# The product with v of some heads: from split one-pass matmuls on the whole array to plain fp32 matmuls on two halves of it

## The chip, the cores and the metric

The kernel runs on one core of a Trainium2 chip. The metric is the device time of one execution in microseconds (us). The engines are named as in the profile: PE is TensorE's matmul, PEld its weight load, DVE VectorE, ACT ScalarE, POOL GpSimd, and SP SyncE, whose queue issues almost all transfers.

## What is computed

Attention with a hashed mask, and then a mixture of four experts that all tokens pass. There are B = 2 batches, H = 8 heads, S = 768 positions and head size D = 64; the experts take rows of 512 and have 1024 hidden units.

```
mask = q_bucket[:, :, :, None] == k_bucket[:, :, None, :]     # 6 sign bits of q @ proj and of k @ proj
scores = where(mask, q @ k.T / sqrt(D), -1e9)
attn = exp(scores - max); attn = attn / (sum(attn) + 1e-9)
x = (attn @ v), heads side by side                            # [1536, 512]
out = sum over e of p[:, e] * (relu(x @ w1[e]) @ w2[e])
```

Everything is fp32. The array multiplies fp32 data in two types here: `F32R`, one pass with fewer bits of each operand kept, and plain `F32`. To reach fp32 with `F32R` operands the kernel splits each operand into a high part and a low part and adds the part-products.

## The kernel before, in words

**The attention loop.** The function `attention` walks over 96 steps i, one for each query tile t of 128 rows, of 16 heads in order (batch 0 first). In each step the string `ORDER = "THXVMSEYNRP"` sets which stages are issued and in which order, each for the tile that lies its own lag behind: S (scores, L401 and L403, and the masked minimum on DVE, L408), E (exponential on ACT, L424), N and R (sums of rows and their reciprocals, through DRAM), P (preparing the next head, and loading the one after), M (scaling by the reciprocals).

**The two ways of turning p.** The product with v needs p transposed. The first 9 heads (b * H + h below `LIGHT_FROM` = 9) do it on PE: stage T transposes with the identity (L470), ACT copies the high part (L474) and DVE makes the low part (L475). The last 7 heads, called light, go through DRAM. Stage X (three steps after S) transposes blocks of 32 x 32 on DVE (L489) and writes them to a DRAM tile `scr` (L493). Stage Y (four steps after) reads it back with four gathering transfers (L502) into a tile `ptlo`. Stage H (six steps after) copies its high part into `pthi` on ACT (L515) and subtracts it in place on POOL (L516).

**The product with v.** Two query tiles form a group g of 256 columns, so a head has three groups. `split_v` (on POOL, L353 and L356, at the head's step 4) makes from v a tile `vv` whose 128 columns per chunk of keys are the high part (64) beside the low part (64). Stage V (`stage_v`, L526) does six matmuls of 256 moving columns with the high part of p in one step (part 0), and six with the low part in the next step (part 1), all into one PSUM bank `pv`. Then ACT copies the 64 rows of the other part into `xtmp` (L546), and DVE adds them to the head's own 64 rows (L551 for light heads, L558 for the others). `LAG_VL` = 7 sets part 0 of light heads seven steps after S.

**The experts beside it.** The experts of batch 0 (`moe`: first layer L775 to L777, second layer L715 to L717) are issued in between the attention steps of batch 1. The ratio is fixed in the program: each stage yields a cost (654 for each part of V, 652 for S, 1960 or 2600 for pieces of the experts), and attention steps are issued until their sum has caught up. After that follow the experts of batch 1 (`moe_fast`). Every engine takes its instructions in the order in which they are written.

**Memory.** `load_v` (L210, on SP's queue) brings v of a head two heads ahead into the pool `ld` (tag `tv`, two slots); `vv` has two slots in the pool `vp`; `pthi` and `ptlo` have two each. PSUM tiles named `one` share four banks (`pv`, `mps`).

Of the kernel before, what the change touches and what calls it, by code (L numbers as in the profile page):

```python
# [8 lines left out]
F32 = mybir.dt.float32  # L9
F32R = mybir.dt.float32r  # L10
ACTF = mybir.ActivationFunctionType
ALU = mybir.AluOpType
PSUM = bass.MemoryType.PSUM

P = 128
# [20 lines left out]
WARM = 2  # L36
W_STEP = 12
PREP_AT = 0
ORDER = "THXVMSEYNRP"
LIGHT_FROM = 9  # L40
LAG_VL = 7
DRAIN = 1000
LAG_X = 3
LAG_Y = 4
LAG_H = 6
SPLIT_FIRST = 3


# [1 line left out]
def tile_lsh_attention__then__domain_moe(  # L50
# [11 lines left out]
    nc = tc.nc  # L62
    B, H, S, D = q.shape
    NB = proj.shape[1]
    E, DM, F = w1.shape
    NT = S // P
# [8 lines left out]
    GN = G * P  # L75
# [8 lines left out]
    ld = ctx.enter_context(tc.tile_pool(name="ld", bufs=2))  # L84
    stk = ctx.enter_context(tc.tile_pool(name="stk", bufs=2))
    vp = ctx.enter_context(tc.tile_pool(name="vp", bufs=2))
# [3 lines left out]
    ptp = ctx.enter_context(tc.tile_pool(name="ptp", bufs=2))  # L90
# [13 lines left out]
    def one(name):  # L104
        return ps1.tile([P, 512], F32, tag="one", name=name)
# [93 lines left out]
    def load_qk(b, h):  # L199
        if in_blocks(b, h):  # L200
            load_blocks(b, h)
            return
        t = ld.tile([P, NT, 2, D], F32, tag="tqk", name="tqk")
        for i, src in enumerate((q, k)):
            nc.sync.dma_start(out=t[:, :, i, :], in_=src[b, h].rearrange("(p c) d -> p c d", c=NT))
        loaded[0, b, h] = t

    def load_v(b, h):
        t = ld.tile([P, NT, D], F32, tag="tv", name="tv")
        nc.sync.dma_start(out=t, in_=v[b, h].rearrange("(p c) d -> p c d", c=NT))  # L210
        loaded[1, b, h] = t

# [133 lines left out]
    vvs = {}  # L346

    def split_v(b, h):
        tv = loaded.pop((1, b, h))
        vv = vp.tile([P, NT, P], F32R, tag="vv", name="vv")  # L350
        vvs[b, h] = vv
        hi, lo = (0, D) if h % 2 == 0 else (D, 0)
        nc.gpsimd.tensor_scalar(  # L353
            out=vv[:, :, hi : hi + D], in0=tv, scalar1=1.0, scalar2=1.0, op0=ALU.mult, op1=ALU.mult
        )
        nc.gpsimd.tensor_tensor(  # L356
            out=vv[:, :, lo : lo + D], in0=tv, in1=vv[:, :, hi : hi + D].bitcast(F32), op=ALU.subtract
        )
# [3 lines left out]
    for j in range(KD):  # L362
        t = xp.tile([P, 2, S], F32R, tag=f"x{j}", name="xs0")
# [14 lines left out]
    pts = {}  # L378
    pvs = {}
    xf = {}  # L380

    def light(b, h):
        return b * H + h >= LIGHT_FROM
# [46 lines left out]
    rows = {}  # L430
# [46 lines left out]
    pxs = {}  # L477
# [27 lines left out]
            )  # L505
        pxs[b, h, g] = (px, lo)

    def stage_h(b, h, g):
        px, lo = pxs.pop((b, h, g))
        hi = ptp.tile([P, NT, GN], F32R, tag="pthi", name="pthi")  # L510
        fh = hi.rearrange("p c n -> p (c n)")
        fl = lo.rearrange("p c n -> p (c n)")
        for a in range(2):
            sl = slice(a * S, (a + 1) * S)
            nc.scalar.activation(fh[:, sl], px[:, sl], ACTF.Copy)  # L515
            nc.gpsimd.tensor_tensor(out=fl[:, sl], in0=px[:, sl], in1=fh[:, sl].bitcast(F32), op=ALU.subtract)  # L516
        view = [x.rearrange("p (a c q) -> p c a q", c=NT, q=32) for x in (fh, fl)]
        pts[b, h, g] = view

    def stage_v(b, h, g, part):  # L520
        vv = vvs[b, h]
        if part == 0:
            pvs[b, h, g] = one("pv")
        ps = pvs[b, h, g]
        for c in range(NT):
            nc.tensor.matmul(  # L526
                ps[:, :GN].rearrange("p (a q) -> p a q", q=32) if light(b, h) else ps[:, :GN],
                vv[:, c],
                pts[b, h, g][part][:, c],
                start=part == 0 and c == 0,  # L530
                stop=part == 1 and c == NT - 1,
            )
        if part == 0:
            return
        pts.pop((b, h, g))
        pvs.pop((b, h, g))
        j, odd = divmod(h, 2)
        if b:
            x = xraw[:, j, g * GN : (g + 1) * GN]
        else:  # L540
            if not odd:
                xf[b, j, g] = xs.tile([P, GN], F32, tag=f"xf{g}", name="xf", bufs=1)
            x = xf[b, j, g]
        mine, other = (slice(0, D), slice(D, P)) if not odd else (slice(D, P), slice(0, D))
        tmp = xs.tile([P, GN], F32, tag="xtmp", name="xtmp")
        nc.scalar.activation(tmp[mine], ps[other, :GN], ACTF.Copy)  # L546
        if XADD_POOL and b == 0:
            nc.scalar.activation(x[mine], ps[mine, :GN], ACTF.Copy)
            nc.gpsimd.tensor_tensor(out=x[mine], in0=x[mine], in1=tmp[mine], op=ALU.add)
        elif light(b, h):  # L550
            nc.vector.tensor_tensor(  # L551
                out=x[mine].rearrange("p (t a q) -> p a t q", t=G, q=32),
                in0=ps[mine, :GN].rearrange("p (a t q) -> p a t q", t=G, q=32),
                in1=tmp[mine].rearrange("p (a t q) -> p a t q", t=G, q=32),
                op=ALU.add,
            )
        else:
            nc.vector.tensor_tensor(out=x[mine], in0=ps[mine, :GN], in1=tmp[mine], op=ALU.add)  # L558
# [20 lines left out]
    def attention():  # L579
        n = len(seq)  # L580
        prep = [iter(())]

        def stage_light(f, j):
            if 0 <= j < n and light(*seq[j][:2]) and j % G == G - 1:
                b, h, t = seq[j]
                f(b, h, t // G)

        def do(op, i):
            if op == "N":
                j = i - LAG_N  # L590
                if 0 <= j < n:
                    stage_n(*seq[j])
            elif op == "R":
                j = i - LAG_R
                if 0 <= j < n:
                    stage_r(*seq[j])
            elif op == "T":
                j = i - LAG_T
                if 0 <= j < n and not light(*seq[j][:2]):
                    stage_t(*seq[j])  # L600
                    return 654
            elif op == "X":
                stage_light(stage_x, i - LAG_X)
            elif op == "H":
                stage_light(stage_h, i - LAG_H)
            elif op == "Y":
                stage_light(stage_y, i - LAG_Y)
            elif op == "S":
                if i < n:
                    b, h, t = seq[i]  # L610
                    if t == 0:
                        x = hseq.index((b, h))
                        prep[0] = prep_head(*hseq[x + 1]) if x + 1 < len(hseq) else iter(())
                    stage_s(b, h, t)
                    return 652
                return DRAIN
            elif op == "V":
                c = None
                for il, lag in enumerate((LAG_V, LAG_VL)):
                    for part in range(G):  # L620
                        j = i - lag - part
                        if 0 <= j < n and j % G == G - 1 and light(*seq[j][:2]) == bool(il):
                            b, h, t = seq[j]
                            stage_v(b, h, t // G, part)
                            c = 654 + (c or 0)
                return c
            elif op == "M":
                for g in range(NT // G):
                    for lag, last in ((LAG_M + g, False), (LAG_V + 1 + G * g + G - NT, True)):
                        j = i - lag  # L630
                        if 0 <= j < n and j % NT == NT - 1 and seq[j][1] % 2:
                            if (seq[j][:2] == (0, H - 1)) == last:
                                stage_m(*seq[j][:2], g)
            elif op == "E":
                j = i - LAG_E
                if 0 <= j < n:
                    stage_e(*seq[j])
            elif op == "P":
                if i < n:
                    b, h, t = seq[i]  # L640
                    c = next(prep[0], None) if t >= PREP_AT else None
                    x = hseq.index((b, h))
                    if t == QK_AT and x + 2 < len(hseq):
                        load_qk(*hseq[x + 2])
                    if t == 4:
                        split_v(b, h)
                        if x + 2 < len(hseq):
                            load_v(*hseq[x + 2])
                    return c
            return None  # L650

        for i in range(n + max(LAG_V, LAG_VL) + G + 1):
            for op in ORDER:
                c = do(op, i)
                if c is not None:
                    yield c
# [338 lines left out]
    with tc.manual_schedule():  # L995
# [7 lines left out]
        i = 0  # L1003
# [17 lines left out]
        for b in range(B):  # L1021
            dm = da = 0.0
            for c in (moe_fast if b else moe)(b, b * NU):
                dm += c
                while da < dm * ATT_PACE * n_att / n_moe:
                    x = next(att, None)
# [34 lines left out]
```

## Time and profile before

| | |
|---|---|
| time, median of 3 runs | 735.47 us (735.18 to 736.24) |
| the profiled execution | 735.63 us, of which 733.9 are the span from first to last instruction |
| busy share of the span | PE 99%, PEld 90%, DVE 70%, ACT 49%, POOL 47% |
| mean granted TensorE clock | 1.000 of full speed |
| product with v, all heads (L526) | 576 matmuls, 88.5 us busy |

Busy times of PE are sums of printed durations without overlap; one matmul is printed with its whole latency, and the next one starts before it ends. A time per instruction is therefore better read from one start to the next. Idle time of an engine other than the one that sets the end costs nothing by itself.

### The profile page before, as it was taken

Reading aid. Unit: us, or ns where it says so; the run is one execution under the profiler, and the core shown is the slowest. Engines: PE = TensorE matmul, PEld = TensorE weight load, DVE = VectorE, ACT = ScalarE, POOL = GpSimd, SP = SyncE. Lnnn points to the kernel's source line nnn. Section 1 sums busy time; section 2 is a strip of 40 time slices with the busy share of each in tenths; the row PEclk is TensorE's granted clock in tenths of the full one; section 3 lists DMA queues with packets and bytes.
Section 4 is the critical chain, followed back from the end, with each engine's and each line's share of the span. In section 5 each row is a group of like instructions: output and inputs, shape, how many; then the busy total and the mean of one; then the engine's idle time right before and its main releaser. Section 6 shows DMA issues by size and latency. Waiting matters only on the chain.

```text
span 733.9 us, 11306 instructions
## 1 busy us (share of the span) xinstructions
PE 723.1 (99%) x4060; PEld 663.6 (90%) x4060; DVE 516.2 (70%) x898; ACT 356.0 (49%) x702; POOL 345.9 (47%) x298
## 2 busy tenths in 40 slices
PE   8899999999999999999999999999999999999998
PEld 6899899998998989989899999898988989899896
DVE  6899999947577766766766433878668586686863
ACT  6999899744444454535444211443435234353430
POOL 6142715422576666675756733844334242343420
PEclk9999999999999999999999999999999999999999
DMA  4555464444989897987776412142121221212202
GB/s 97 152 128 121 92 159 102 115 106 120 239 207 239 240 222 206 223 236 205 215 212 208 112 58 84 56 147 87 58 58 59 84 87 48 68 58 82 92 0 87
DMA packets 77272, 94.86 MB, mean 129 GB/s; under 512 B 38712, under 2 KB 51960, under 8 KB 77216
## 3 DMA queue, kind: packets, MB, share of 16 engines
q1 hardware_dynamic: 76192, 93.81, 46.8%
q8 instruction: 32, 0.52, 0.3%
q10 hardware_dynamic: 1024, 0.33, 0.2%
q14 instruction: 24, 0.20, 0.1%
HBM read 62.68 MB, written 19.71 MB: 112 GB/s over the span
## 4 chain that ended last, share of the span: by engine, by line
PE 87%; DVE 6%; ACT 3%; DMA 2%; issue 1%; POOL 1%; SPq 0%; ACTq 0%; DVEq 0%; POOLq 0%
PE mps L717 12%; PE mps L715 12%; PE mps L716 12%; PE pv L526 6%; PE mps L775 6%; PE mps L777 6%; PE mps L776 6%; PE sps L403 3%; PE sps L401 3%; DVE p L408 3%; PE mps L931 2%; PE mps L927 2%; PE mps L930 2%; PE ptps L470 2%; DVE ptlo L475 2%; PE hps L317 2%
## 5 line engine op out<-in xcount | busy, mean ns | idle before, releaser
L717 PE MATMUL mps<-w2hi,hl 128*128 128x512 f32 (+1 forms) x388 | 151.1, 389 | 0.0
L715 PE MATMUL mps<-w2hi,hh 128*128 128x512 f32 (+1 forms) x388 | 151.0, 389 | 0.0
L716 PE MATMUL mps<-w2lo,hh 128*128 128x512 f32 (+1 forms) x388 | 150.7, 388 | 0.0
L709 DVE SCALAR_TENSOR_TENSOR acc<-mps,pe,acc 128x512 f32<-128x512 f32 (+1 forms) x85 | 63.0, 741 | 64.4 <-PE mps L717 64.4
L424 ACT ACTIVATE p<-p,nb 128x768 f32<-128x768 f32 x96 | 89.6, 933 | 26.4 <-DVE p L408 25.8
L516 POOL TENSOR_TENSOR ptlo<-ptlo,pthi 128x768 fp32r<-128x768 f32 x42 | 77.4, 1864 | 48.8 <-ACT pthi L515 44.8
L408 DVE TENSOR_SCALAR_CACHE_REDUCE p<-sps 128x768 f32<-128x768 f32 x96 | 90.6, 945 | 1.5 <-PE sps L403 0.7
L913 POOL TENSOR_TENSOR w2lo<-ws,w2hi 128x512 fp32r<-128x512 f32 x32 | 40.8, 1297 | 105.9 <-ACT w2hi L912 105.9
L717 PEld LDWEIGHTS mps<-w2hi,hl 128*128 128x128 f32 x388 | 72.9, 188 | 17.1 <-DVE hl L946 1.3
L775 PE MATMUL mps<-xs,w1hi 128*128 128x384 f32 x256 | 86.5, 338 | 0.0
L777 PE MATMUL mps<-xs,w1lo 128*128 128x384 f32 x256 | 86.1, 336 | 0.0
L776 PE MATMUL mps<-xs,w1hi 128*128 128x384 f32 x256 | 86.0, 336 | 0.0
L782 ACT ACTIVATE hh<-mps 128x384 fp32r<-128x384 f32 x64 | 31.4, 490 | 112.2 <-PE mps L777 112.0
L716 PEld LDWEIGHTS mps<-w2lo,hh 128*128 128x128 f32 x388 | 73.0, 188 | 13.5
L715 PEld LDWEIGHTS mps<-w2hi,hh 128*128 128x128 f32 x388 | 72.9, 188 | 13.0
L783 DVE SCALAR_TENSOR_TENSOR hl<-mps,hh 128x384 fp32r<-128x384 f32 x64 | 35.4, 553 | 52.2 <-ACT hh L782 51.7
L685 POOL TENSOR_TENSOR w1lo<-ws,w1hi 128x512 fp32r<-128x512 f32 x32 | 42.5, 1332 | 43.6 <-DVE w1hi L692 17.0
L685 POOL TENSOR_TENSOR w2lo<-ws,w2hi 128x512 fp32r<-128x512 f32 x32 | 42.6, 1333 | 37.5 <-DVE w2hi L692 25.9
L475 DVE TENSOR_TENSOR ptlo<-ptps,pthi 128x384 fp32r<-128x384 f32 x108 | 54.5, 545 | 7.5 <-ACT pthi L474 7.2
L872 POOL TENSOR_TENSOR w1lo<-ws,w1hi 128x512 fp32r<-128x512 f32 x24 | 38.3, 1612 | 35.9 <-ACT w1hi L868 29.2
L401 PE MATMUL sps<-ah,q 128*128 128x384 f32 x192 | 50.1, 342 | 2.3 <-DVE p L408 2.1
L403 PE MATMUL sps<-k,al 76*128 76x384 f32 x192 | 50.4, 342 | 0.7 <-DVE k L263 0.4
(139 smaller groups left out, 1558.0 us busy)
## 6 DMA issues: line engine op xcount, KB each, us to landing
ws<-in_moe_w_dram SPq DMA_DIRECT2D x64, 512.0 KB
scr<-t SPq DMA_DIRECT2D x21, 768.0 KB
ptlo<-scr SPq DMA_DIRECT2D x84, 192.0 KB
q<-ah SPq DMA_DIRECT2D x28, 192.0 KB
tv<-in_v_dram SPq DMA_DIRECT2D x16, 192.0 KB
k<-ah SPq DMA_DIRECT2D x15, 192.0 KB
rdb<-row SPq DMA_DIRECT2D x15, 192.0 KB
out_dram<-acc SPq DMA_DIRECT2D x11, 256.0 KB
```

The lines of the kernel that those rows point to most:

```text
L401: nc.tensor.matmul(ps[:, i, :NH], q1[:, sl], k1[:, i * NH : (i + 1) * NH], start=True, stop=False)
L403: nc.tensor.matmul(ps[:, i, :NH], q2[0:MQE, sl], k2[0:MQE, i * NH : (i + 1) * NH], start=False, stop=True)
L408: nc.vector.tensor_scalar(out=two(pt), in0=ps[:, :, :NH], scalar1=MASKED, scalar2=MASKED, op0=ALU.min, op1=ALU.min, accum_out=nb,)
L424: nc.scalar.activation(pt, pt, ACTF.Exp, bias=nb, scale=-1.0, accum_out=dens[b, h, r][:, o : o + 1])
L516: nc.gpsimd.tensor_tensor(out=fl[:, sl], in0=px[:, sl], in1=fh[:, sl].bitcast(F32), op=ALU.subtract)
L685: nc.gpsimd.tensor_tensor(out=lo[:, c - 1], in0=st[c - 1], in1=hi[:, c - 1].bitcast(F32), op=ALU.subtract)
L715: nc.tensor.matmul(ps, hh[:, ts], w2hi[:, f, cs], start=n == 0, stop=False)
L716: nc.tensor.matmul(ps, hh[:, ts], w2lo[:, f, cs], start=False, stop=False)
L717: nc.tensor.matmul(ps, hl[:, ts], w2hi[:, f, cs], start=False, stop=n == FC - 1)
L775: nc.tensor.matmul(ps[:, :SB], w1hi[:, kk, fs], xhi[b, kk][:, sl], start=kk == 0, stop=False)
L776: nc.tensor.matmul(ps[:, :SB], w1hi[:, kk, fs], xlo[b, kk][:, sl], start=False, stop=False)
L777: nc.tensor.matmul(ps[:, :SB], w1lo[:, kk, fs], xhi[b, kk][:, sl], start=False, stop=kk == KD - 1)
```

## The change

For light heads stage H goes away, and v is not split. The tile `ptlo`, as the transfers bring it, is the moving operand in plain fp32, and v as loaded is the standing operand, 64 columns per chunk of keys. The six chunks go by turns to the left and the right half of the array's columns (`tile_position` (0, 0) and (0, 64)), so that the even chunks add up in PSUM rows 0 to 63 and the odd ones in rows 64 to 127. The add of the two halves after it (L546, L551) is as before. All six matmuls are issued in the step of part 0, and none in the step of part 1. Because v as loaded is now read by PE, `load_v` puts it by turns into `tv` and `vv` slots. The 9 other heads stay as they are.

```diff
--- before.py
+++ after.py
@@ -36,13 +36,12 @@
 WARM = 2
 W_STEP = 12
 PREP_AT = 0
-ORDER = "THXVMSEYNRP"
+ORDER = "TXVMSEYNRP"
 LIGHT_FROM = 9
 LAG_VL = 7
 DRAIN = 1000
 LAG_X = 3
 LAG_Y = 4
-LAG_H = 6
 SPLIT_FIRST = 3
 
 
@@ -206,7 +205,9 @@
         loaded[0, b, h] = t
 
     def load_v(b, h):
-        t = ld.tile([P, NT, D], F32, tag="tv", name="tv")
+        x = b * H + h - LIGHT_FROM
+        pool, tag = (vp, "vv") if x >= 0 and x // 2 % 2 else (ld, "tv")
+        t = pool.tile([P, NT, D], F32, tag=tag, name="tv")
         nc.sync.dma_start(out=t, in_=v[b, h].rearrange("(p c) d -> p c d", c=NT))
         loaded[1, b, h] = t
 
@@ -347,6 +348,9 @@
 
     def split_v(b, h):
         tv = loaded.pop((1, b, h))
+        if light(b, h):
+            vvs[b, h] = tv
+            return
         vv = vp.tile([P, NT, P], F32R, tag="vv", name="vv")
         vvs[b, h] = vv
         hi, lo = (0, D) if h % 2 == 0 else (D, 0)
@@ -505,35 +509,39 @@
             )
         pxs[b, h, g] = (px, lo)
 
-    def stage_h(b, h, g):
-        px, lo = pxs.pop((b, h, g))
-        hi = ptp.tile([P, NT, GN], F32R, tag="pthi", name="pthi")
-        fh = hi.rearrange("p c n -> p (c n)")
-        fl = lo.rearrange("p c n -> p (c n)")
-        for a in range(2):
-            sl = slice(a * S, (a + 1) * S)
-            nc.scalar.activation(fh[:, sl], px[:, sl], ACTF.Copy)
-            nc.gpsimd.tensor_tensor(out=fl[:, sl], in0=px[:, sl], in1=fh[:, sl].bitcast(F32), op=ALU.subtract)
-        view = [x.rearrange("p (a c q) -> p c a q", c=NT, q=32) for x in (fh, fl)]
-        pts[b, h, g] = view
-
     def stage_v(b, h, g, part):
         vv = vvs[b, h]
-        if part == 0:
-            pvs[b, h, g] = one("pv")
-        ps = pvs[b, h, g]
-        for c in range(NT):
-            nc.tensor.matmul(
-                ps[:, :GN].rearrange("p (a q) -> p a q", q=32) if light(b, h) else ps[:, :GN],
-                vv[:, c],
-                pts[b, h, g][part][:, c],
-                start=part == 0 and c == 0,
-                stop=part == 1 and c == NT - 1,
-            )
-        if part == 0:
-            return
-        pts.pop((b, h, g))
-        pvs.pop((b, h, g))
+        if light(b, h):
+            if part == 1:
+                return
+            ps = one("pv")
+            px = pxs.pop((b, h, g))[0].rearrange("p (a c q) -> p c a q", c=NT, q=32)
+            for c in range(NT):
+                rows = slice(c % 2 * D, (c % 2 + 1) * D)
+                nc.tensor.matmul(
+                    ps[rows, :GN].rearrange("p (a q) -> p a q", q=32),
+                    vv[:, c],
+                    px[:, c],
+                    start=c < 2,
+                    stop=c >= NT - 2,
+                    tile_position=(0, c % 2 * D),
+                )
+        else:
+            if part == 0:
+                pvs[b, h, g] = one("pv")
+            ps = pvs[b, h, g]
+            for c in range(NT):
+                nc.tensor.matmul(
+                    ps[:, :GN],
+                    vv[:, c],
+                    pts[b, h, g][part][:, c],
+                    start=part == 0 and c == 0,
+                    stop=part == 1 and c == NT - 1,
+                )
+            if part == 0:
+                return
+            pts.pop((b, h, g))
+            pvs.pop((b, h, g))
         j, odd = divmod(h, 2)
         if b:
             x = xraw[:, j, g * GN : (g + 1) * GN]
@@ -601,8 +609,6 @@
                     return 654
             elif op == "X":
                 stage_light(stage_x, i - LAG_X)
-            elif op == "H":
-                stage_light(stage_h, i - LAG_H)
             elif op == "Y":
                 stage_light(stage_y, i - LAG_Y)
             elif op == "S":
```

## Rows read from the trace of the kernel before

**Rows 1.** The page: span, engines' busy time (us, share, instructions), granted clock by slices.

```profile
span 733.9 us, 11306 instructions
...
PE 723.1 (99%) x4060; PEld 663.6 (90%) x4060; DVE 516.2 (70%) x898; ACT 356.0 (49%) x702; POOL 345.9 (47%) x298
...
PEclk9999999999999999999999999999999999999999
```

**Rows 2.** Busy time of each engine by windows (us), 175 to 425 us.

```profile
175.00:425.00 250.00, 250.00 (x1385) 232.95 (x1385) 167.93 (x287) 109.38 (x202) 161.09 (x116) 1.00 0.79 210
```

**Rows 3.** The chain of waits, by line, 175 to 425 us.

```profile
by line: PE pv L526 12.7%; PE mps L717 12.5%; PE mps L715 12.5%; PE mps L775 12.5%; PE mps L776 12.5%; PE mps L716 12.4%; PE mps L777 12.4%; PE sps L403 5.3%; PE sps L401 5.2%; PE hps L317 2.1%
```

**Rows 4.** Groups of instructions by shape, 175 to 425 us: busy us, mean ns | idle before.

```profile
L516 POOL TENSOR_TENSOR ptlo<-ptlo,pthi 128x768 fp32r<-128x768 f32 x42 | 77.4, 1864 | 48.8 <-ACT pthi L515 44.8 <-PE pv L526 4.0
...
L515 ACT ACTIVATE pthi<-ptlo 128x768 fp32r<-128x768 f32 x42 | 33.1, 836 | 30.1 <-DMA ptlo<-scr 29.9
...
L526 PE MATMUL pv<-ptlo,vv 128*128 128x256 f32 x133 | 19.7, 283 | 0.0
L526 PE MATMUL pv<-pthi,vv 128*128 128x256 f32 x132 | 19.4, 282 | 0.0
...
L356 POOL TENSOR_TENSOR vv<-tv,vv 128x384 fp32r<-128x384 f32 x6 | 6.3, 1045 | 0.5
...
L353 POOL TENSOR_SCALAR vv<-tv 128x384 fp32r<-128x384 f32 x6 | 3.1, 511 | 0.2
```

**Rows 5.** PE in order of time (start us, us busy, line), 302 to 312.5 us.

```profile
304.33 0.40 PE L715 MATMUL mps<-w2hi,hh 128*128 128x512 f32 x1
...
306.86 0.40 PE L717 MATMUL mps<-w2hi,hl 128*128 128x512 f32 x1
307.09 0.88 PE L526 MATMUL pv<-ptlo,vv 128*128 128x256 f32 x6
307.81 0.52 PE L401 MATMUL sps<-ah,q 128*128 128x384 f32 x2
```

**Rows 6.** PE in order of time, 33.5 to 36 us, heads turned on PE.

```profile
33.70 0.82 PE L298 MATMUL tps<-ident,tqk 128*128 128x128 f32 x6
34.36 0.82 PE L470 MATMUL ptps<-ident,p 128*128 128x128 f32 x6
34.93 0.96 PE L526 MATMUL pv<-ptlo,vv 128*128 128x256 f32 x6
35.73 0.52 PE L401 MATMUL sps<-ah,q 128*128 128x384 f32 x2
```

**Rows 7.** Weight loads in order of time, 304 to 308 us.

```profile
304.16 0.19 PEld L715 LDWEIGHTS mps<-w2hi,hh 128*128 128x128 f32 x1
```

**Rows 8.** ACT in order of time, 393 to 426 us, with what it waited for.

```profile
393.91 1.56 ACT L515 ACTIVATE pthi<-ptlo 128x768 fp32r<-128x768 f32 x2
...
413.53 1.58 ACT L515 ACTIVATE pthi<-ptlo 128x768 fp32r<-128x768 f32 x2 [8.38 <-DMA ptlo<-scr]
```

**Rows 9.** PE in order of time, the pv bursts that follow those two copies.

```profile
397.66 0.88 PE L526 MATMUL pv<-pthi,vv 128*128 128x256 f32 x6
...
418.40 0.88 PE L526 MATMUL pv<-pthi,vv 128*128 128x256 f32 x6
```

**Rows 10.** Waits of SP's queue: us in total, times, longest us.

```profile
SPq L343 <- POOL vv L353: 14.5, 9, 4.6
...
SPq L210 <- POOL vv L356: 11.6, 5, 7.4
```

## The prediction

> **What bounds the kernel now.** I read the busy shares first: the tensor engine (PE) is busy for 99% of the span at full granted clock [rows 1]. That alone proves nothing, because the ends of pipelined matmuls are modelled, so I looked at the stretch in which the changed code runs. The heads turned through DRAM ("light" heads, the last 7 of 16) have their scores and products between about 175 and 425 us. In that stretch PE has no idle time, while POOL works 161 of 250 us, ACT 109 and DVE 168 [rows 2]. The chain of waits says the same: in that stretch it consists of PE lines alone, and the product with v (L526) is 12.7% of it [rows 3]. The groups of instructions show no idle time before any pv matmul [rows 4]. So here the kernel is a queue of matmuls, each issued as soon as the array takes it. Time falls only when PE gets less to stream, and it rises by whatever PE gets more; what ACT and POOL lose is worth nothing by itself.
>
> **Prices on PE.** I take the distance from start to start, not the printed duration, which includes the pipeline's latency. Six pv matmuls of 256 moving columns start at 307.09, and the next instruction starts at 307.81: 0.72 us, or 0.120 each. Twelve matmuls of 512 columns run from 304.33 to 307.09: 0.230 each [rows 5]. The difference gives 0.110/256 = 0.43 ns per column and 0.010 us per instruction, for these one-pass operands (the fp32r type).
>
> **What the change removes.** There are 7 light heads with 3 groups of two query tiles, so 21 groups. Each now has 12 one-pass matmuls, in two bursts of six: 2 x 0.72 = 1.44 us, for all groups 30.2 us of PE. ACT loses 42 copies of 0.836 us (35 us), POOL 42 subtractions of 1.864 (78 us) and 7 splits of v of 0.511 + 1.045 (11 us) [rows 4]. On PE's path the relief of ACT and POOL is worth 0: PE waits for neither in that stretch [rows 2, 4]. I find no later stage that inherits it either, since the order on PE is written out and PE stays the chain.
>
> **What it adds on PE.** Each group gets 6 matmuls in plain fp32: 64 columns of v as the standing operand, 256 moving columns, on the left and right half of the array by turns. No plain fp32 product of two full operands stands in the trace of before. The nearest row is the plain fp32 transpose: six of 128 columns take 33.70 to 34.36, so 0.110 each [rows 6], where one pass of 128 columns would be 0.128 x 0.43 + 0.010 = 0.065. Taking off the fixed part, that is 0.100 against 0.055, about two passes. A product needs more, because the other operand has two parts as well: the old code spends four part-products (high and low of p against high and low of v) to reach fp32. So I bound one new matmul by 2 passes (512 columns, 0.230) from below and by four separate issues (4 x 0.120 = 0.48) from above. I take four passes in one instruction: 1024 x 0.43 + 10 ns = 0.45 us, since the four part-products are what the kernel before needed. The Trainium skill, "FP8 and Floating Point Precision", section TensorE Precision Notes, says that true fp32 takes four passes through the array; by it the sum stays as taken, and no run here shows it yet.
>
> Six of these in a row are 2.70 us; if the two halves really run at the same time, 1.35 us. Nothing in this trace divides the array, so both ends stay open: 1.35 (paired) and 2.70 (one after the other, up to 2.88 with four issues each). Paired, the columns that stream are the same number as before: 3 pairs x 4 x 256 = 12 x 256. I take paired, because different output columns and different PSUM partitions share nothing that a row of this trace shows to be a limit. The Trainium skill, "TensorE: Matmul & The Clock Gate", section Measured speedup vs the span model, gives 2.38 times for three column tiles; an estimate from it for two is 2 x 2.38/3 = 1.59, so 2.70/1.59 = 1.70 us per group and +5.5 us in all. No run here shows it.
>
> **Changing over.** Twice per group the array goes from whole to halves and back. Below: nothing, as changes between fp32 transposes and fp32r matmuls leave no gap (33.70 to 35.73: 12 transposes and 6 pv matmuls in 2.03 us, where 12 x 0.110 + 0.72 = 2.04) [rows 6]. Above: the array empties and the next weights are loaded only then. The tail is 0.283 - 0.120 = 0.16 us [rows 4, 5]; a weight load leads its matmul by 304.33 - 304.16 = 0.17 [rows 5, 7]. So 0.33 per change, 0.66 per group. I take the tail alone, 2 x 0.16 = 0.33: none of the free changes altered which parts of the array work together, and the weight load can go ahead on the idle half. The Trainium skill, "TensorEngine Tiling (Array Packing)", section Key Properties, says that a change of tiling mode drains the engine; by that rule the sum is the one with the tail in it, and without the rule it would be 1.35 alone.
>
> **What moves.** All six matmuls are now issued in the step of part 0 and none in the step of part 1, where the old code put six in each. The pacing costs that the generator hands out are the same, so the rest of PE's order stays; the pv bank is held for one burst instead of two steps, which PE did not wait for anyway. A wait moves too: ACT used to take the wait for the four gathering transfers (up to 8.38 us), now PE's first pv matmul does, and all of PE queues behind it. But PE comes to it later: ACT began its copy, so the data was there, at 393.91 and 413.53, PE its pv burst at 397.66 and 418.40 [rows 8, 9]. The smallest such margin over the 21 groups is that first one, 3.75 us, so the wait costs 0; without the margin it would cost PE the whole lateness. The v tile is now held until PE has read it, not only until POOL has split it. The load that reuses a slot is issued four steps after its last reader's step or later, so SP should not block there, and SP loses part of its waits for POOL's splits (14.5 and 11.6 us over all heads) [rows 10]. Worth 0 on PE.
>
> **Sum.** Per group 1.35 + 0.33 - 1.44 = +0.24 us; 21 groups: +5.0 us. The profiled execution took 735.63 us, of which 733.9 are the span; so 740.6, and against the median 735.47 it is **740.5 us**, 0.7% slower. A difference under 0.2% (1.5 us) can't be told from no change here.
>
> **Rivals and chances.**
>
> (A) Paired, with changes that cost next to nothing. Then a group costs 1.35 to about 1.51, and the total moves by -1.9 to +1.5 us: 733.6 to 737. For it: the free changes of [rows 6], and equal streamed columns. Against it: the halves must start together; if the second waits for part of the first, half an instruction (0.22 us) hangs over at the end of a group. It ends faster when three pairs with both changes cost under 1.44 us, so a pair under 0.48. Chance 0.30, of which 0.19 is faster by over 0.2%.
>
> (B) The forecast: paired, with changes that cost 0.16 to 0.66 per group: 737 to 748, likeliest 740.5. Chance 0.32.
>
> (C) The halves do not overlap, because matmuls start and end in order and a fp32 product occupies the engine until its last pass. A group costs 2.70 to 2.88, so +1.26 to +1.44 us, 21 times: +26.5 to +30 us, 762 to 766, and up to 779 with the dear changes. For it: everything in the trace runs one matmul after the other. Against it: nothing in the trace could have overlapped. Chance 0.26.
>
> (D) A plain fp32 matmul takes two passes as the transpose does, and the pairs overlap: 6 x 0.230/2 = 0.69 per group, -0.75 x 21 = -16 us, 720 us. For it: [rows 6]. Against it: the transpose multiplies by an exact identity. Chance 0.08.
>
> (E) PE stalls at its new wait for the gathering transfers: if they land 5 us later than now, the tightest group loses 1.25 us; if every group had the margin of the tightest, 26 us. Against it: the transfers do not change, and ACT's copy no longer stands behind them. Chance 0.04.
>
> The likeliest single number is B's, 740.5; A and B together span 733.6 to 748. The range that leaves out no more than 2 in 10 has to take in C without dear changes: 732.5 to 764. Left out are D, and the upper part of C (about 0.1). Faster: 0.19 + 0.08 = 0.27. Same: the rest of A, 0.11, and a little of B, 0.03: 0.14. Slower: 0.59.
>
> **What the profile of the changed kernel will show.** The distance from the first pv matmul of a burst to the next other PE instruction decides everything: 1.35 means A, about 1.7 B, 2.7 C, 0.7 D. Starts of neighbouring pv matmuls in pairs (or evenly 0.22 apart) mean overlap; 0.45 apart means none. A gap before the first pv matmul and after the last shows what a change costs. POOL should lose some 89 us of busy time and ACT 35 with PE still without idle time from 175 to 425; if the span moves by anything but 21 times the change in a burst, a wait has appeared, and the waits of PE would name the transfers or a bank. The prediction fails if the halves take turns, or if plain fp32 streams at another rate than four times one pass.

## The result, and the profile after

The changed kernel takes 740.29 us (median of 3 runs, 739.85 to 740.75) against 735.47: the ratio is 1.0063, 95% interval 1.0041 to 1.0086. It is slower by 4.8 us; the forecast was 740.5. The two profiled spans differ by 738.5 - 733.9 = 4.6 us.

The page of the changed kernel, with the lines that answer to [rows 1]:

```profile
span 738.5 us, 11094 instructions
...
PE 727.9 (99%) x4060; PEld 649.3 (88%) x4060; DVE 502.6 (68%) x898; ACT 324.3 (44%) x660; POOL 256.0 (35%) x242
...
PEclk9999999999999999999999999999999999999999
```

POOL lost 90 us of work and ACT 32, and yet the time went up with PE's busy time (+4.8). The number of matmul records is the same as before, 4060, although the code issues half as many instructions for the products of the light heads: one plain fp32 matmul is two records. The stretch of the light heads by windows of busy time, the answer to [rows 2]:

```profile
175.00:425.00 250.00, 250.00 (x1364) 213.49 (x1363) 152.76 (x282) 76.47 (x158) 69.55 (x60) 1.00 0.78 208
```

PE is still without idle time there; POOL went from 161 to 70 us. The groups of instructions in that stretch, the answer to [rows 4]:

```profile
L521 PE MATMUL pv<-ptlo,tv 128*64 128x256 f32 x252 | 31.8, 388 | 0.0
...
L521 PEld LDWEIGHTS pv<-ptlo,tv 128*64 128x64 f32 x252 | 16.2, 136 | 12.4 <-issue 5.7 <-DVE al L231 0.4 <-DMA row<-rt 0.4
```

There are 252 records of 64 columns for 21 x 6 = 126 instructions. Now one burst, PE in order of time (first column the start, second the busy time):

```profile
299.89 0.34 PE L783 MATMUL mps<-xs,w1lo 128*128 128x384 f32 x1
300.16 1.51 PE L521 MATMUL pv<-ptlo,tv 128*64 128x256 f32 x12
301.60 0.44 PE L781 MATMUL mps<-xs,w1hi 128*128 128x384 f32 x1
301.88 0.34 PE L782 MATMUL mps<-xs,w1hi 128*128 128x384 f32 x1
```

A 384-column matmul holds PE for 0.174 us in this stretch (299.54 to 299.71 to 299.89 just before). From the start of L783 to the second start after the burst are 301.88 - 299.89 = 1.99 us, of which the two neighbours' own 2 x 0.174 are to be taken off: the group costs PE 1.645 us (the starts in nanoseconds give 269 + 1445 + 278 - 348 = 1644). Before it was 2 x 0.717 = 1.434. The same view, cut off ever later, shows how many records of this burst have started by 300.3, 300.5 and 300.7 us (the last number of a row):

```profile
300.16 0.44 PE L521 MATMUL pv<-ptlo,tv 128*64 128x256 f32 x2
...
300.16 0.65 PE L521 MATMUL pv<-ptlo,tv 128*64 128x256 f32 x4
...
300.16 0.87 PE L521 MATMUL pv<-ptlo,tv 128*64 128x256 f32 x6
```

They start two by two. The distances between the 12 starts, in nanoseconds, and the distance from the last to the next instruction:

```
6, 260, 7, 209, 7, 209, 7, 209, 6, 210, 6 | 309
```

So a pair takes 216 ns, the two halves of the array start 6 to 7 ns apart, and six pairs stream in 6 x 0.216 = 1.296 us. The rest, 1.645 - 1.296 = 0.349, are the two changes: 0.095 between the end of L783's own time and the first start, 0.05 more in the first pair (6 + 260 where others have 216), 0.10 after the last pair (6 + 309) and 0.10 in the instruction after it (0.278 for 0.174). The weight loads show the same places:

```profile
300.15 1.06 PEld L521 LDWEIGHTS pv<-ptlo,tv 128*64 128x64 f32 x12 [0.25 <-issue]
301.60 0.19 PEld L781 LDWEIGHTS mps<-xs,w1hi 128*128 128x128 f32 x1 [0.39 <-DVE al L231]
301.71 0.19 PEld L782 LDWEIGHTS mps<-xs,w1hi 128*128 128x128 f32 x1
```

The weight load that used to lead its matmul by 0.17 us [rows 7] now starts with it, before the burst and after it; within the burst the loads lead again. The producer named in the second row cannot be the reason, since the gap returns at every burst. After the burst the next load starts 0.11 us later (301.60, 301.71), and the first matmul holds PE 0.10 us longer than usual; before it, the second load of a half starts 0.055 us after the first, and the first pair takes 0.05 us longer. So each change reads as two parts: some 0.095 us in which nothing new starts, and then a weight load that the first matmul has to wait for, 0.05 us for 64 columns going in and 0.10 for 128 coming out. This is a reading of the records; no run takes the two parts apart.

All 21 bursts look like this (1.445 or 1.446 us from the first start to the next instruction). 21 x (1.645 - 1.434) = 4.4 us, which is the difference of the spans but for 0.2. That 0.2 is a remainder of larger ones: in the profiled run of the changed kernel the first score matmul starts 0.9 us later (8.98 us against 8.04), and from the first to the last matmul of the experts it takes 3.9 us more (590.3 against 586.5), where the bursts alone give 4.4. What the other matmuls gained there was not traced.

### The profile page after: what moved, and what is told of

The parts are those of the page before. It is cut to its first block, busy times and chain, and to the rows that moved or that the text cites. A ratio compares the mean times of both kernels' runs of the same rounds, so it can differ in the third digit from the quotient of the medians.

```text
span 738.5 us, 11094 instructions
## 1 busy us (share of the span) xinstructions
PE 727.9 (99%) x4060; PEld 649.3 (88%) x4060; DVE 502.6 (68%) x898; ACT 324.3 (44%) x660; POOL 256.0 (35%) x242
## 3 DMA queue, kind: packets, MB, share of 16 engines
q10 hardware_dynamic: 1024, 0.33, 0.2%
## 4 chain that ended last, share of the span: by engine, by line
PE 86%; DVE 5%; ACT 4%; DMA 2%; issue 1%; POOL 1%; SPq 0%; ACTq 0%; DVEq 0%; POOLq 0%
PE mps L721 12%; PE mps L723 12%; PE mps L722 12%; PE mps L781 6%; PE mps L783 6%; PE mps L782 6%; PE pv L521 4%; PE sps L405 3%; PE sps L407 3%; PE mps L937 2%; PE mps L933 2%; PE mps L936 2%; PE pv L534 2%; DVE p L412 2%; ACT p L428 2%; PE ptps L474 2%
## 5 line engine op out<-in xcount | busy, mean ns | idle before, releaser
L412 DVE TENSOR_SCALAR_CACHE_REDUCE p<-sps 128x768 f32<-128x768 f32 x96 | 90.9, 949 | 1.8 <-PE sps L407 1.0
L783 PE MATMUL mps<-xs,w1lo 128*128 128x384 f32 x256 | 86.0, 336 | 0.0
L781 PEld LDWEIGHTS mps<-xs,w1hi 128*128 128x128 f32 x256 | 48.0, 188 | 4.1 <-DVE hl L789 2.3
```

The costliest lines, as they stand in the source:

```text
L412: nc.vector.tensor_scalar(out=two(pt), in0=ps[:, :, :NH], scalar1=MASKED, scalar2=MASKED, op0=ALU.min, op1=ALU.min, accum_out=nb,)
L781: nc.tensor.matmul(ps[:, :SB], w1hi[:, kk, fs], xhi[b, kk][:, sl], start=kk == 0, stop=False)
L783: nc.tensor.matmul(ps[:, :SB], w1lo[:, kk, fs], xhi[b, kk][:, sl], start=False, stop=kk == KD - 1)
```

## Experiments

Each kernel ran beside the kernel before on the same chip; a ratio is to the kernel before.

**The work of ACT and POOL put back, unread.** The copies and subtractions come back in their old places and sizes, and write a tile that nothing reads.

```diff
...
+    def stage_h(b, h, g):
+        px, lo = pxs[b, h, g]
+        hi = ptp.tile([P, NT, GN], F32R, tag="pthi", name="pthi")
+        fh = hi.rearrange("p c n -> p (c n)")
+        for a in range(2):
+            sl = slice(a * S, (a + 1) * S)
+            nc.scalar.activation(fh[:, sl], px[:, sl], ACTF.Copy)
+            nc.gpsimd.tensor_tensor(out=fh[:, sl], in0=px[:, sl], in1=fh[:, sl].bitcast(F32), op=ALU.subtract)
...
```

> The copies on ACT and the subtractions on POOL come back with the same sizes and places as in the kernel before, into a tile that nothing reads; PE's work is that of the changed kernel. Theory (PE never waits for ACT or POOL there, so their relief was worth nothing): 740.3 us, within 1 us. Rival (the relief was worth some us, and the loss on PE is larger than it looks): slower than 740.3 by 2 us or more.

740.34 us, ratio 1.0055 (1.0042 to 1.0067). By windows of busy time, 175 to 425 us:

```profile
175.00:425.00 250.00, 250.00 (x1362) 213.50 (x1362) 166.93 (x283) 107.02 (x200) 149.65 (x101) 1.00 0.78 208
```

ACT is back at 107 us and POOL at 150 of the 161 us before (the splits of v were not put back), and the time stays. The relief was worth nothing here, and it hides no larger loss.

**The changes doubled.** Two pairs of chunks in the step of part 0, the third pair in the step of part 1, with other matmuls in between.

```diff
-            for c in range(NT):
+            for c in (range(4), range(4, NT))[part]:
...
```

> Chunks 0 to 3 in the step of part 0, chunks 4 and 5 in the step of part 1, so that the array is divided and joined twice per group. Theory (each pair of changes costs 0.345 us): 21 x 0.345 = +7.2 us, about 747.5 us, and the gaps before and after the second burst are as long as those of the first. Rival (the gap before a burst is PE's wait for the gathered p or for a bank): the second burst has its operands already and comes without gaps, 740 to 741 us.

747.80 us, ratio 1.0157 (1.0139 to 1.0174). PE in order of time around a second burst:

```profile
402.80 0.34 PE L787 MATMUL mps<-xs,w1lo 128*128 128x384 f32 x1
403.06 0.65 PE L521 MATMUL pv<-ptlo,tv 128*64 128x256 f32 x4
403.65 0.45 PE L785 MATMUL mps<-xs,w1hi 128*128 128x384 f32 x1
403.93 0.34 PE L786 MATMUL mps<-xs,w1hi 128*128 128x384 f32 x1
```

The second burst needs no new data and no new bank, and it has the same price: 403.93 - 402.80 - 0.348 = 0.78 us, of which 2 x 0.216 stream; 0.35 are left. So the gaps are the price of changing over, and no wait for data.

**Plain fp32 on the whole array.** The standing operand is 128 columns, two neighbouring chunks of v, so that the array is never divided. Rows 64 to 127 of the bank do not hold the right sums, and the output is not the reference's.

```diff
+                two_c = slice(c // 2 * 2, c // 2 * 2 + 2)
                 nc.tensor.matmul(
-                    ps[rows, :GN].rearrange("p (a q) -> p a q", q=32),
-                    vv[:, c],
+                    ps[:, :GN].rearrange("p (a q) -> p a q", q=32),
+                    vv[:, two_c].rearrange("p c d -> p (c d)"),
                     px[:, c],
...
-                    tile_position=(0, c % 2 * D),
```

> Plain fp32 on the whole array: the standing operand is 128 columns (two neighbouring chunks of v side by side), six matmuls one after the other; rows 64 to 127 of the bank, and so the output, do not hold the right sums. Theory (four passes of 256 columns each, and the changes are paid for dividing the array, not for plain fp32): 6 x 0.432 = 2.59 us per group with no gaps around it, against 1.645 with them, +0.95 x 21 = +20 us: about 760 us. Rival (the gaps belong to the change between fp32r and plain fp32): 2.59 + 0.345, about 767 us.

759.38 us, ratio 1.0313 (1.0299 to 1.0327). PE in order of time:

```profile
204.87 0.34 PE L782 MATMUL mps<-xs,w1lo 128*128 128x384 f32 x1
205.04 2.75 PE L521 MATMUL pv<-ptlo,tv 128*128 128x256 f32 x12
207.44 0.52 PE L780 MATMUL mps<-xs,w1hi 128*128 128x384 f32 x1
207.81 0.34 PE L781 MATMUL mps<-xs,w1hi 128*128 128x384 f32 x1
```

From 204.87 to 207.81 less 0.348 are 2.59 us, which is 12 x 0.216: no gap before, none after. (The first matmul after the burst is recorded as starting early and lasting long; the sum over both shows that nothing was lost.) Two things follow. A plain fp32 matmul of 256 columns takes 2 x 0.216 = 0.43 us, about four times the 0.110 us that 256 columns of one pass stream. And plain fp32 among one-pass matmuls costs no change; dividing the array does. (A standing operand of fewer columns is not enough for it: L317 with its 108, in the kernel before, holds PE for the usual 0.174 us.)

**The two halves not by turns.** Chunks 0 to 2 on the left half, then 3 to 5 on the right.

```diff
-                rows = slice(c % 2 * D, (c % 2 + 1) * D)
+                half = c // (NT // 2)
+                rows = slice(half * D, (half + 1) * D)
...
```

> Chunks 0 to 2 go to the left half of the array and chunks 3 to 5 to the right half, instead of by turns. Theory (only neighbours in the order of issue overlap): only chunks 2 and 3 can run together, so a burst streams 5 x 0.432 us instead of 3 x 0.432; +0.86 us per group, 21 groups, +18 us: about 758 us. Rival (each half works off its own queue, however the matmuls are ordered): the burst stays 1.45 us from its first start to the next instruction, and the time at 740.3.

751.11 us, ratio 1.0199 (1.0185 to 1.0213): between the two, and neither theory holds as it was put. How many records of a burst have started by 305.95, 306.2 and 306.4 us:

```profile
305.83 0.43 PE L522 MATMUL pv<-ptlo,tv 128*64 128x256 f32 x1
...
305.83 0.65 PE L522 MATMUL pv<-ptlo,tv 128*64 128x256 f32 x2
...
306.10 0.65 PE L522 MATMUL pv<-ptlo,tv 128*64 128x256 f32 x3
```

The last row begins with a later record, because the first had ended by then: by 306.4 four have started, at 305.83, 306.10, 306.316 and 306.322. The first two are alone; then a second stream sets in, and from there each stream goes on every 0.216 us by itself, 0.056 apart. The burst is eight such places long instead of six (1.928 us for 1.445): the right half begins at the third place of the left one and takes six. The fourth record to start has the longer duration of the first one (430 ns against 379), which in all bursts marks the first record of a half; it starts 6 ns after the third, and two records of the same half never start less than 0.2 us apart in the other bursts. Read so, the right half's first record started while the left half's fourth to sixth, which stand before it in the code, had not: the halves do not wait for each other's order, but here the engine did not look farther ahead than some four records.

**Two by two.** To test that reading: chunks 0, 2 (left), 1, 3 (right), 4, 5.

```diff
-            for c in range(NT):
+            for c in (0, 2, 1, 3, 4, 5):
```

> The chunks in the order 0, 2 (left), 1, 3 (right), 4 (left), 5 (right). With all left chunks first, the right half started 4 records late and ran on its own from then on. Theory (each half takes its own matmuls in order, and the engine sees some 4 records ahead): two left chunks in front delay the right half by nothing, a burst stays 1.45 us from its first start to the next instruction, 740.3 us. Rival (only neighbours overlap): 4 x 0.432 instead of 3 x 0.432 us, +9 us, about 749.

740.71 us, ratio 1.0051 (1.0036 to 1.0065): the burst stays in pairs (13 to 14 ns apart now) and 1.453 us long. The reading holds for a distance of four records; how the engine does it was not tested further.

**One burst per head.** The products of the three groups are issued together, in the step of the third; the gathered p waits in the slots of `pthi` too, and the scaling of batch 1 moves one step later.

```diff
+        n_y[0] += 1
+        tag = ("ptlo", "pthi")[n_y[0] % 2]
-        lo = ptp.tile([P, NT, GN], F32R, tag="ptlo", name="ptlo")
+        lo = ptp.tile([P, NT, GN], F32R, tag=tag, name="ptlo")
...
+        elif part == 0 and g == NT // G - 1:
+            for x in range(NT // G):
+                stage_v1(b, h, x, 0)
```

> The products of all three groups of a light head are issued in one burst, in the step of the third group; the gathered p waits in the slots that the high parts left free. Theory (a burst costs 0.345 us for dividing and joining the array, whatever its length): 7 bursts instead of 21 save 14 x 0.345 = 4.8 us, about 735.5 us, which is the time of the kernel before. Rival (three banks are held at once and the experts' matmuls wait for one): PE shows idle time behind the bursts, and the time stays near 740.

735.46 us where the kernel before took 736.87 on that chip: ratio 0.9982 (0.9973 to 0.9990). Its span is 732.5 us, 6.0 below the changed kernel's, 4.8 expected; 1.0 of it lies in the start, since its first score matmul begins at 7.97 us and not at 8.98, and from the first to the last matmul of the experts it is 5.1 us shorter. PE in order of time:

```profile
383.06 0.34 PE L791 MATMUL mps<-xs,w1lo 128*128 128x384 f32 x1
383.33 4.11 PE L529 MATMUL pv<-ptlo,tv 128*64 128x256 f32 x36
387.36 0.45 PE L789 MATMUL mps<-xs,w1hi 128*128 128x384 f32 x1
387.64 0.34 PE L790 MATMUL mps<-xs,w1hi 128*128 128x384 f32 x1
```

387.64 - 383.06 - 0.348 = 4.23 us for 18 pairs of 0.216 = 3.89; 0.34 are left, once per head. PE shows no wait for a bank. By the two ratios this version is faster than the changed kernel by 0.8%; it is faster than the kernel before by 0.2%, which is about the least that can be told from no difference.

**One more head through DRAM: the kernel before, the changed one, and the one with one burst per head.** In each the only edit is this.

```diff
-LIGHT_FROM = 9
+LIGHT_FROM = 8
```

> The kernel before with one more head turned through DRAM. Theory (PE sets the end; POOL, with 161 of 250 us busy, still has room): -36 x 0.109 = -3.9 us, about 731.6 us. Rival (POOL's subtractions fill it and PE waits for the low parts): 735.5 us or more; then the relief of POOL is what lets more heads go through DRAM.

> The changed kernel with 8 heads through DRAM instead of 7, a burst for each group as it stands. Theory (without the copies and subtractions p is ready as soon as it lands, so the extra head does not stall PE at the point where the experts set in, other than by what the three-group kernel with 8 heads showed, some 3.5 us): -3.9 - 0.4 + 3 x 0.345 + 3.5 us, about 740.5 us. Rival (the loss of 7 us that the kernel before took with 8 heads comes from the transfers and the order, which are the same here): about 747 us, with PE waiting before its first light product.

> As the kernel with three groups in a burst, and one more head is turned through DRAM (8 instead of 7). Theory (PE sets the end, ACT and POOL now have room): the head loses 36 transposes of 0.109 us on PE, and its product goes from 3 x 1.434 to 3 x 1.296 + 0.345 us: -4.0 us, about 731.5 us, faster than the kernel before by 0.5%. Rival (the transfers, already busy for about 0.8 of this stretch, become the limit): PE waits for the gathered p, and the time stays at 735.5 or goes above.

The kernel before becomes slower: 743.73 us, ratio 1.0098 (1.0085 to 1.0111). The changed one stays: 740.70 us, ratio 1.0066 (1.0052 to 1.0079). So does the one with a burst per head: 735.15 us, ratio 0.9986 (0.9974 to 0.9998). The kernel before with 8 heads, by windows and by what PE waited for in order of time:

```profile
150.00:175.00 25.00, 22.07 (x121) 21.72 (x120) 11.63 (x22) 11.06 (x21) 12.82 (x11) 0.90 0.85 199
```

```profile
167.09 0.98 PE L526 MATMUL pv<-pthi,vv 128*128 128x256 f32 x6 [2.93 <-ACT pthi L515]
```

The changed kernel with 8 heads, the same window:

```profile
150.00:175.00 25.00, 25.00 (x145) 22.45 (x144) 12.36 (x24) 10.28 (x21) 1.29 (x2) 1.00 0.94 232
```

In the first PE waits 2.93 us for ACT's copy of the high part, and the mean granted clock of the window falls to 0.90; 3.4 us of it, from 1.5 us after that wait on, are at the lower level of 1.2 GHz. The copy was late because the gathered p was: for 1.3 us of the wait it had not landed, then the two copies took 1.6 us. Rows of the same run:

```profile
150.98 3.65 POOL L516 TENSOR_TENSOR ptlo<-ptlo,pthi 128x768 fp32r<-128x768 f32 x2 [4.88 <-ACT pthi L515]
...
156.61 1.30 POOL L685 TENSOR_TENSOR w2lo<-ws,w2hi 128x512 fp32r<-128x512 f32 x1
```

```profile
SPq L674 <- POOL w2lo L685: 7.0, 1, 7.0
```

```profile
158.43 1.83 SPq L502 DMA_DIRECT2D ptlo<-scr  x4
```

```profile
165.46 1.58 ACT L515 ACTIVATE pthi<-ptlo 128x768 fp32r<-128x768 f32 x2 [3.25 <-DMA ptlo<-scr]
```

For the group before, POOL's subtraction waited 4.88 us for ACT's copy; the split of expert weights (L685) stood behind it on POOL, a load of expert weights (L674) waited 7.0 us on SP's queue for that split, and the gather (L502) stood behind the load. In the second kernel the copies and subtractions are gone, SP has no such wait, the same gather is issued at 151.15 instead of 158.43 us, and PE doesn't wait in this window. So here the work taken off ACT and POOL is worth something, by its places in the queues more than by its busy time. The rival of the first kernel (POOL full, PE waiting for the low parts) had the direction but not the reason: POOL works 12.8 of these 25 us, and PE waits for a high part. The chain is read from one run of each kernel and was not tested by itself.

But the gain of 4 us that fewer transposes promised doesn't arrive in any of the three. PE waits more just before the experts set in: from 125 to 150 us it is busy for 21.94, 22.10 and 21.48 us, where the kernel before has 24.18. With a burst per head it waits there, among others, twice 1.1 us for DVE's pass over the scores (L412). The full clock of the second kernel, too, holds only for the window shown: in the profiled runs of the first two kernels the granted clock stood at the lower level for 6.8 us, from 144.7 and 143.3 us on, after the first two of these waits. In that of the third it did not, but its longer runs (up to 737.9 us, the shortest 733.5) show a mean granted clock down to 0.993. In neither of the two changed kernels does PE wait for the gathered p, so the transfers, the rival of the third, are not what takes the gain. What it would take to fill that place was not tried. The window for the first, the second and the third kernel:

```profile
125.00:150.00 25.00, 21.94 (x138) 19.93 (x137) 21.53 (x46) 16.45 (x36) 8.73 (x11) 0.89 0.57 155
...
125.00:150.00 25.00, 22.10 (x132) 20.14 (x131) 21.77 (x47) 15.71 (x34) 9.91 (x13) 0.87 0.62 171
...
125.00:150.00 25.00, 21.48 (x145) 19.58 (x144) 21.93 (x46) 17.21 (x37) 10.31 (x13) 1.00 0.63 175
```

## Why the prediction was right

**The bound.** PE is the chain, before and after, and the time moved by what the bursts on PE moved by. Putting ACT's and POOL's work back changed nothing, as forecast.

**Four passes, paired.** Taken: 0.45 us for one matmul, 1.35 for three pairs. Measured: 0.432 and 1.296, which is 0.42 ns for each of 1024 columns with no fixed part left, where 0.43 ns and 10 ns were taken. That the halves would run together was a choice between two values with no row behind it; the measurement bears it out. The Trainium skill, "FP8 and Floating Point Precision", section TensorE Precision Notes, states four passes; the trace agrees, with 12 x 0.216 us for six matmuls of 256 columns on the whole array. The overhang of half an instruction that rival A was charged with does not occur, as two records of different halves start 7 ns apart. What rival C (no overlap) would have cost is shown by the whole-array kernel, without the changes: 759.4 us, 2.6 below the lower end that was worked out for C.

**The changes.** Taken: 0.33 us per group; measured about 0.35 in the bursts of three kernels. The size came out right, but in part by luck: with the records read as above, two errors cancel. The prediction charged the emptying alone, 0.16 each time, and let the weight load go ahead on the idle half. In the trace the load does not go ahead: it starts together with the first matmul, before the burst and after it. By that reading its wait costs 0.05 and 0.10 us, and the gap ahead of it only 0.095 each time, so 0.145 going in and 0.20 coming out. That is the course of the upper bound (first emptying, then loading), at about half of its 0.33 each time. The Trainium skill, "TensorEngine Tiling (Array Packing)", section Key Properties, says that a change of mode drains the engine; the price fits it, with about 0.35 us for each burst, twice that for two bursts, and none where the array stays whole, but that the array runs empty in the gap is not seen in the records, whose ends are modelled. Rival A, which charged next to nothing, was wrong in this one term.

**The sign.** The distance from the first pv matmul of a burst to the next other PE instruction was to decide between A (1.35) and B (about 1.7). It is 1.445, nearer to A. The sign was put wrongly: 0.095 us of the price lie ahead of the first pv matmul and 0.10 in the instruction after the burst, and only the whole group, 1.645, tells B from A.

**The sum.** +0.24 us per group was forecast and +0.21 measured; 21 groups give +5.0 and +4.4 us. The medians differ by 4.8 and the spans by 4.6, so 0.2 to 0.4 us lie elsewhere, in the start of the profiled run and in the other matmuls.

**The moved wait and v's slots.** PE waits for nothing from 175 to 425 us, so the margin of 3.75 us sufficed (E). Among the waits of SP's queue none for L521 appears.

**The rate (D).** Two passes for a whole product is ruled out by the whole-array kernel.

## What to carry to other kernels

Where one engine is the chain, cost a rewrite on that engine alone: here 120 us of work taken from two others were worth nothing until, with one more head, they stood in the way of a transfer that PE waited for. Two column halves do run plain fp32 at twice the rate, but each visit to the divided array costs about 0.35 us, so divided matmuls belong together in long bursts: one of 36 records instead of three of 12 turned a loss of 0.6% into a gain of 0.2%. Issue the halves by turns; putting three matmuls of one half first makes a burst a third longer (1.93 us for 1.45).

## What was not expected of the hardware

One plain fp32 matmul is two records of 0.216 us each for 256 columns, and records of two instructions on different halves interleave. With the left half's three matmuls first, the right half's first started three records after the burst began, ahead of three that stand before it in the code, if the long first duration is read as above. The Trainium skill, "TensorE: Matmul & The Clock Gate", section The mechanism, says that matmuls start and end in program order; this trace speaks against it for the starts on two column halves, and there the instructions are not taken in the order in which they are written, as the description of the kernel before has it for every engine. From the 2.38 times for three column tiles in its section Measured speedup vs the span model the prediction estimated 1.59 for two halves; measured are 2.59/1.296 = 2.0 inside a burst, and 2.59/1.645 = 1.57 for a burst of three pairs with its changes.
